# Moving the 64-feature products of the first batch's first MLP half next to the second batch's recurrent groups

## The chip, the core and the metric

The kernel runs on one core of a Trainium2 chip. The metric is the device time of one execution in microseconds (us), as the median of several runs. Engines are named as in the profile: PE is TensorE (matrix products), PEld its weight loads, DVE is VectorE, ACT is ScalarE, POOL is GpSimd, SP is SyncE (here it issues all DMAs).

## The reference

For four batches of 768 tokens, an mLSTM cell with 8 heads of 40 features runs over the tokens and gives x (768 x 320 for each batch). Then x goes through a Fourier mix, a normalization and an MLP with a residual:

```python
C = f_stab * C + i_stab * outer(v, k)          # per head, token by token
n = f_stab * n + i_stab * k
y = sigmoid(o) * (C @ q) / max(|n . q|, 1)     # x: the heads side by side
u = x + real(fft(fft(x, axis=1), axis=2))
un = (u - mean(u)) / sqrt(var(u) + 1e-6)
out = u + max(un @ w_ch1, 0) @ w_ch2           # 320 -> 1280 -> 320
```

All of it is float32. The change concerns `un @ w_ch1` of the first batch only.

## The kernel before, in words

**Recurrence.** The token loop is rewritten into chunks of 128 tokens (6 to a batch); within a chunk all is matrix products, masks and scales, and a small state passes from chunk to chunk. From the second batch on, a chunk is worked as two halves of 64 tokens, with products on 64x64 quarters of the array (line 519, a helper, issues all of them). For chunk c of a batch that starts at slot s0, with s = s0 + 3c, the products stand in this order:

- slot s: `halves_scores` (keys by queries) and `halves_to_state` (what the chunk adds to the state, tile ps). The DVE adds these to the state in `halves_add` (L665, L667).
- slot s+3: `halves_from_state` and `halves_from_chunk(..., 0)` (tile ph); then `halves_between` (L699), a one-element copy by ACT that reads ph; then `halves_from_chunk(..., 1)`, the other half of those products, which PE starts only when that copy is done.

Slot s+3 of chunk c is slot s of chunk c+1, so from the second chunk on the products of two chunks stand together on PE. The text calls such a bunch a recurrent group. Between them `halves_weigh` (L672) has DVE multiply scores by the weights W, which ACT exponentiates (L491) and POOL masks (L515). `mlstm_finish` (L712 to L720, DVE) and `mlstm_tanh` (L605, ACT) end a chunk.

**Fourier mix.** `mix_feat` (L938) makes the mixed features in the tile pu, `mix_add` (L952 to L966, DVE) adds them, `mix_center` (L974, ACT), `mix_turn` (L981, PE transposes) and `mix_turn_out` (L986, ACT) give uT, the features by tokens. `mix_rstd` and `mix_rstd_step` (L994 to L1008) find 1/sqrt(var) on DVE and POOL.

**First MLP half of the first batch.** A group `gr` is 384 tokens (two groups), and f counts ten blocks of 128 hidden features. A product has 320 input features: 128, 64 and 128. The two products over 128 features fill the array (L1059, in `mlp_in`). The product over the 64 middle features fills half of its rows; for two neighbouring f (a pair, n = f // 2) the two run on the upper and the lower half of the rows (L1050, in `between`, inside `mlp_in`). Each float32 product is two instructions in the profile. A pair needs two PSUM banks (tile pm), and `mlp_relu` (L1074, ACT) empties them into h. `bank` hands out four PSUM banks by a written list (`turn`), in the order of requests; pu, put (the transposes), pm and po (the second MLP half, L1184) take from it.

In gr 0, `between` follows each pair's other products. In gr 1, the 64-feature products of pairs 1 and 3 are issued ahead, together with those of pairs 0 and 2.

**Weights.** w1 and w2 arrive as 64-bit floats in pieces (raw) and are converted: DVE splits the words (L406, L408), ACT scales them (L413, L414), DVE joins them (L420 to L426). These conversions stand in the queues of DVE and ACT among the other work of the stretch.

**What sets the order.** A plan: `at(slot, phase, function, ...)` collects the calls, and they are issued sorted by slot and then by phase (EVAC 0, FILL 1, MAIN 2, FILL_PE 3, plus fractions). Each engine takes its instructions in that order and waits on semaphores. For the first batch's MLP, slot 31 + 10 gr + f holds `mlp_in(gr, f)` at MAIN, and the second batch's chunks start at slots 32, 35, 38, 41, 44 and 47. With FILL_PE, the recurrent group of a slot stands after that slot's `mlp_in`. The last chunk's first part stands at MAIN - 0.1 of slot 50, ahead of `mlp_in(1, 9)`.

Of the kernel before, what the change touches and what calls it, by code (L numbers as in the profile page):

```python
# [14 lines left out]
AF = mybir.ActivationFunctionType  # L15
# [4 lines left out]
L = 128  # L20
# [8 lines left out]
NFF = DFF // L  # L29
TAIL = DM - 2 * L  # L30
TG = NT // 2
# [22 lines left out]
def kernel(  # L54
# [14 lines left out]
    nc = tc.nc  # L69
# [18 lines left out]
    def bank(name, shape, n=None):  # L88

        return ps_m.tile(shape, FP, name=name, tag=f"pm{next(turn) if n is None else n}")  # L90
# [14 lines left out]
    w1_sb = const.tile([L, 2, DFF], FP, name="w1_sb")  # L105
    w1t_sb = const.tile([L, DFF // 2], FP, name="w1t_sb")
    w2_sb = const.tile([L, NFF, DM], FP, name="w2_sb")
    uT_bufs = [const.tile([L, 3, TG, L], FP, name=f"uT{n}") for n in range(2)]
# [15 lines left out]
    def at(slot, phase, fn, *args):  # L124
        plan.setdefault((slot, phase), []).append((fn, args))
# [7 lines left out]
    EVAC, FILL, MAIN, FILL_PE = range(4)  # L133
# [248 lines left out]
    class Piece:  # L382
        def __init__(self, dst, src):
            self.dst, self.src, self.float = dst, src, src.dtype == FP
# [377 lines left out]
    def plan_halves(b, s0, stride=3):  # L762
        for c in range(NT):
            s = s0 + stride * c
            t = 22 + 2 * c if b == 1 and c < 3 else s - 5
            at(t, FILL, mlstm_load, b, c)
            at(t, FILL, mlstm_load_max, b, c)
            at(34 if b == 1 and c == 2 else t + 1, FILL, mlstm_load_decay, b, c)
            at(s - 1, FILL, mlstm_load_o, b, c)
            at(s - 1, FILL, mlstm_scale_v, b, c)  # L770
            at(s - 1, FILL + 0.3, mlstm_exp, b, c, 0)
            at(s, FILL, mlstm_exp, b, c, NP)
            at(s, FILL_PE + 2.05, halves_scores, b, c)
            at(s, FILL_PE + 2.5, halves_to_state, b, c)
            for i in range(2):
                at(s + i, FILL + 0.05, halves_decay, b, c, i)
                at(s + 1 + i, FILL - 0.2, halves_add, b, c, i)
            at(s, FILL + 0.1, mlstm_scale_q, b, c)
            at(s + 1, FILL, mlstm_mask, b, c)
            if (b, c) == (3, 2):  # L780
                at(s + 2, MAIN + 0.1, halves_weigh, b, c)
            else:
                at(s + 1, FILL + 0.55 if b == 1 and c > 0 else MAIN + 0.7, halves_weigh, b, c)
            end = c == NT - 1
            at(s + 3, MAIN - 0.1 if end else FILL_PE, halves_from_state, b, c)
            at(s + 3, MAIN - 0.1 if end else FILL_PE, halves_from_chunk, b, c, 0)
            at(s + 3, MAIN if end else FILL_PE + 0.5, halves_between, b, c)
            at(s + 3, FILL_PE + 3, halves_from_chunk, b, c, 1)
            at(s + 3, FILL_PE + 0.6, mlstm_tanh, b, c)
            at(s + (5 if (b, c) == (2, 2) else 4), {(2, 4): FILL + 0.3, (3, 3): FILL - 0.3}.get((b, c), FILL + 0.3 if b == 1 else MAIN + 0.55), mlstm_finish, b, c)  # L790
            at(s + 6, FILL - 0.6, halves_rows, b, c)
# [3 lines left out]

    class Mix:
        def __init__(self):
            self.pu, self.uc, self.pt, self.po = {}, {}, {}, {}

    mixes = {}  # L800

# [239 lines left out]
    def mlp_in(b, gr, f):  # L1041


        k = mixes[b]
        u = [uT_bufs[gr][:, ch].rearrange("p c t -> p (c t)") for ch in range(3)]

        def between(pm, n, start):
            for i in range(2):
                r = slice(i * TAIL, (i + 1) * TAIL)
                nc.tensor.matmul(pm[i], w1t_sb[r, n * L:(n + 1) * L], u[1][r], start=start, stop=not start,  # L1050
                                 skip_group_check=True)


        ahead = gr == 1 and f // 2 in (1, 3)
        if f % 2 == 0:
            k.pm = k.pm_next if ahead else [bank("pm", [L, TG * L]) for _ in range(2)]
        for i, ch in ((1, 1),) if f % 2 else ((0, 0), (0, 1), (1, 0)):
            f0 = (f // 2 * 2 + i) * L
            nc.tensor.matmul(k.pm[i], w1_sb[:, ch, f0:f0 + L], u[2 * ch], start=(ch == 0 and not ahead),  # L1059
                             stop=(ch == 1 and ahead), skip_group_check=True)  # L1060
        if f % 2 and not ahead:
            between(k.pm, f // 2, False)
            if gr == 1 and f // 2 < NFF // 2 - 1:
                k.pm_next = [bank("pm", [L, TG * L]) for _ in range(2)]
                between(k.pm_next, f // 2 + 1, True)


    hid = {}
# [1 line left out]
    def hidden(gr, f):  # L1070
        return hid[gr, f % 2][:, f // 2 * TG * L:(f // 2 + 1) * TG * L]

    def mlp_relu(b, gr, f):
        nc.scalar.activation(out=hidden(gr, f), in_=mixes[b].pm[f % 2], func=AF.Relu, scale=-1.0)  # L1074

# [193 lines left out]
    def plan_mlp(b, s):  # L1271
        groups = range(NT // TG)
        for i in range(NFF // 2) if b > 0 else ():
            for step in range(4):
                at(s, MAIN, mlp_block, b, i, step)
                s += 1
            end = i == NFF // 2 - 1
            for n, (gr, f) in enumerate(((1, 2 * i + 1), (1, 2 * i), (0, 2 * i))):
                at(*((s - 1, MAIN + (-0.1 if gr else 0.1)) if end else (s + n, MAIN + 0.5)), mlp_relu_in_place, gr, f)
        for gr in groups if b == 0 else ():  # L1280
            for f in range(NFF):
                at(s, MAIN, mlp_in, b, gr, f)
                s += 1
                if f % 2:
                    at(s, EVAC, mlp_relu, b, gr, f - 1)
                    at(s, EVAC, mlp_relu, b, gr, f)
        if b > 0:
            for j in range(1, 5):
                at(s - (5, 4, 3, 3)[j - 1], FILL_PE + 0.3, hidden_sums, 0, (j,), 0, NFF // 2 - 2)
            at(s, EVAC, hidden_sums, 0, (1, 2), NFF // 2 - 2, NFF // 2)  # L1290
            at(s, MAIN + 0.1, hidden_sums, 0, (3, 4), NFF // 2 - 2, NFF // 2)
        for n in range(TG) if b > 0 else ():
            for step in range(4):
                at(s, MAIN, mlp_out_pair, b, n, step)
                if n < TG - 1 and step > 1:
                    for j in (2 * step - 3, 2 * step - 2):
                        at(s, MAIN + 0.6, hidden_sums, n + 1, (j,))
                s += 1
        for gr in groups if b == 0 else ():
            for n, (half, i) in enumerate(((0, 0), (0, 1), (0, 2), (1, 0), (1, 1), (1, 2)) if gr == 0 else  # L1300
                                          ((0, 0), (1, 0), (0, 1), (1, 1), (0, 2), (1, 2))):
                at(s, MAIN, mlp_out, b, gr, i, half)
                s += 1
                if half == 1:
                    at(s, EVAC, mlp_store, b, gr, i)
# [6 lines left out]
    def plan_batch(b, s_mlstm, s_mix, s_mlp):  # L1312
        (plan_halves if b > 0 else plan_mlstm)(b, s_mlstm)
        done = [s_mlstm + n for n in ((16, 19, 22) if b == 0 else (18, 21, 22))]
        assert s_mix >= done[-1] and s_mlp >= s_mix + 9
        late = [s_mlp + 2 * c for c in range(TG)]
        if b == 0:
            feat = [s_mix + 1, s_mix + 1, s_mlp + 3]
            turn = [s_mix + 2, s_mix + 3, s_mix + 4]
            add = turn + [s_mlp, s_mlp + 4, s_mlp + 5]  # L1320
            late = [s_mlp + 2, s_mlp + 5, s_mlp + 7]
        else:
            feat = [s_mix + c for c in ((3, 4, 6) if b == 1 else (3, 4, 7))]
            add = [s_mix + c for c in ((4, 4, 5, 6, 7, 7), (4, 5, 5, 6, 8, 9), (4, 4, 5, 6, 8, 9))[b - 1]]
            turn = [s_mix + c for c in ((5, 6, 6) if b == 1 else (6, 7, 8))]
            late = [s_mix + c for c in ((7, 8, 8) if b == 1 else (9, 10, 10))]
            at(s_mlp, EVAC + 0.5, mlp_sums, 0, 3 if b == 2 else 4)
            if b == 2:
                at(s_mlp + 1, MAIN + 0.6, mlp_sums, 3, 4)
        plan_mix(b, s_mix, done, feat, add, turn + late)  # L1330
        s = s_mlp + NFF + 2
        at(s, FILL + 0.6, mix_rstd, b)
        for n in range(3):
            at(s + 3 * n if b == 0 else s, FILL + 0.65, mix_rstd_step, b)
        plan_mlp(b, s_mlp)

    s_mlp = 31
# [154 lines left out]
```

## Time and profile before

| | |
|---|---|
| median of 3 runs | 391.72 us (391.14 to 392.08) |
| the profiled execution | 392.19 us, its span 390.4 us |
| granted TensorE clock | 0.999 |
| PE busy | 379.6 us, 97% of the span |
| DVE, ACT, POOL busy | 278.0, 172.1, 134.9 us |
| L1059, 80 instructions | 59.5 to 110.1 us, 486 ns median |
| L1050, 40 instructions | 62.3 to 111.0 us, 483 ns median |
| L519 of chunks 0 to 5 of batch 2 | in the same stretch |

The span is from the first to the last instruction of the profiled execution; the time of an execution holds a little more. The profile's times are in us from the start of the span. A row of the timeline gives the start, the time up to the last end in the row, the engine, the line and operation, the tiles as out<-in, the shape and the number of instructions; in square brackets stands how long the engine was idle before the row and what ended that. Durations of products overlap, since they are pipelined: how long they hold the array is read from the starts.

### The profile page before, as it was taken

The page shows a single profiled execution, that of the slowest core. Times are in us where ns is not written, and L with a number is a line of the kernel's source. Part 1 is how long each engine was busy: PE and PEld are TensorE (multiplying, and loading weights), DVE is VectorE, ACT ScalarE, POOL GpSimd, SP SyncE. Part 2 cuts the span into 40 slices and gives each one's busy share as a digit, 9 for nine tenths or more (in the row PEclk, how much of TensorE's full clock was granted, in tenths as well). Part 3 has the DMA queues.
Part 4 walks back from the last instruction along what each step waited for, and adds up shares of the span by engine and source line. Part 5 has one row for each costly group of instructions (what it writes and reads, how often), then busy time and mean ns, then how long its engine had stood idle before and what let it go on. Part 6 is the DMA issues. An engine that isn't in the chain of part 4 may idle for free.

```text
span 390.4 us, 10585 instructions
## 1 busy us (share of the span) xinstructions
PE 379.6 (97%) x4174; PEld 277.3 (71%) x4174; DVE 278.0 (71%) x671; ACT 172.1 (44%) x481; POOL 134.9 (35%) x237
## 2 busy tenths in 40 slices
PE   8999899999999999999999999999999999999996
PEld 6777555656667777765569998755588996556996
DVE  7789988499599587476975699777655785346652
ACT  6887357477543233655462314554530133545000
POOL 5739504467954442173254134541500000020000
PEclk9999999999999999999999999999999999999999
DMA  7887499579394345437700626400000000000101
GB/s 224 287 235 204 159 254 255 179 214 271 109 231 116 122 116 150 149 102 184 182 2 28 174 80 192 135 20 2 0 2 34 6 30 34 2 0 0 35 34 35
DMA packets 25631, 44.78 MB, mean 115 GB/s; under 512 B 5727, under 2 KB 14766, under 8 KB 25454
## 3 DMA queue, kind: packets, MB, share of 16 engines
q1 hardware_dynamic: 25582, 44.11, 38.9%
q8 instruction: 33, 0.54, 0.6%
q14 instruction: 16, 0.13, 0.1%
HBM read 38.49 MB, written 4.12 MB: 109 GB/s over the span
## 4 chain that ended last, share of the span: by engine, by line
PE 78%; DVE 14%; issue 3%; ACT 3%; POOL 1%; DVEq 0%; ACTq 0%; POOLq 0%
PE po L1240 20%; PE pm L1121 15%; PE po L1184 8%; PE pm L1059 7%; PE ph L519 4%; PE pm L1126 4%; PE pu L938 4%; PE ps L519 3%; PE pm L1050 2%; PE put L981 2%; PE pz L907 1%; PE pz L895 1%; DVE h L1130 1%; DVE so L716 1%; PE pM L221 1%
## 5 line engine op out<-in xcount | busy, mean ns | idle before, releaser
L1190 DVE SCALAR_TENSOR_TENSOR x<-po,rstd,x 128x160 f32<-128x160 f32 (+1 forms) x69 | 27.1, 394 | 37.4 <-PE po L1240 32.5
L1130 DVE TENSOR_TENSOR h<-h,pm 128x384 f32<-128x384 f32 x60 | 30.5, 548 | 27.1 <-PE pm L1121 12.6
L652 POOL TENSOR_TENSOR C<-C,decB 128x164 f32<-128x164 f32 x30 | 15.9, 531 | 67.5 <-DVE C L667 56.1
L1121 PE MATMUL pm<-uT,w_sb 128*128 128x384 f32 x90 | 37.7, 506 | 1.3 <-DVE uT L1109 0.6
L491 ACT ACTIVATE W<-W,colT 128x64 f32<-128x64 f32 x144 | 37.5, 339 | 0.4 <-DMA W<-M_d 0.4
L1184 PE MATMUL po<-w_sb,h 128*128 128x320 f32 x120 | 34.3, 435 | 0.0
L515 POOL TENSOR_SCALAR_AFFINE_SELECT W<-W 64x512 f32<-64x512 f32 x36 | 27.3, 759 | 10.6 <-ACT W L491 9.1
L1005 POOL TENSOR_TENSOR t<-rstd 128x6 f32<-128x6 f32 x12 | 3.3, 273 | 79.9 <-DVE v L999 79.4
L1059 PE MATMUL pm<-uT,w_sb 128*128 128x384 f32 x80 | 29.2, 500 | 0.1
L1184 PEld LDWEIGHTS po<-w_sb,h 128*128 128x128 f32 x120 | 22.3, 190 | 9.5 <-issue 0.6
L1240 PE MATMUL po<-T,S 128*128 128x160 f32 x180 | 27.8, 301 | 0.3 <-DVE x L1190 0.3
L501 POOL TENSOR_TENSOR qg<-qk,Gb 128x512 f32<-128x512 f32 (+1 forms) x21 | 27.1, 1290 | 1.7 <-DMA qk<-in_qkT 1.6
L1240 PEld LDWEIGHTS po<-T,S 128*128 128x128 f32 x180 | 25.5, 190 | 1.7 <-DVE x L1190 0.5
L1121 PEld LDWEIGHTS pm<-uT,w_sb 128*128 128x128 f32 x90 | 15.5, 189 | 15.6 <-DVE h L1130 6.7
L1240 PE MATMUL po<-w_sb,h 128*128 128x160 f32 x180 | 26.3, 300 | 0.0
L1240 PEld LDWEIGHTS po<-w_sb,h 128*128 128x128 f32 x180 | 25.2, 190 | 1.4 <-DVE x L1190 0.3
L986 ACT COPY uT<-put 128x384 f32<-128x384 f32 x24 | 11.2, 477 | 30.1 <-PE put L981 30.1
L507 POOL TENSOR_TENSOR vw<-kvt,colT 128x328 f32<-128x328 f32 x23 | 19.7, 859 | 13.1 <-DMA qk<-in_qkT 10.1
L1177 ACT ACTIVATE h<-h 128x384 f32<-128x384 f32 x45 | 23.1, 520 | 2.0 <-DVE h L1130 2.0
L1126 PE MATMUL pm<-uT,w1t_sb 64*128 64x384 f32 x120 | 23.4, 508 | 0.0
L1059 PEld LDWEIGHTS pm<-uT,w_sb 128*128 128x128 f32 x80 | 14.1, 189 | 9.6 <-issue 1.9
L974 ACT ACTIVATE uc<-x 128x384 f32<-128x384 f32 x24 | 14.4, 613 | 12.6 <-DVE x L966 11.1
(241 smaller groups left out, 843.4 us busy)
## 6 DMA issues: line engine op xcount, KB each, us to landing
kvt<-in_kv SPq DMA_DIRECT2D x24, 336.0 KB
qk<-in_qkT SPq DMA_DIRECT2D x48, 160.0 KB
raw<-in_w SPq DMA_DIRECT2D x10, 640.0 KB
Gb<-G_d SPq DMA_DIRECT2D x36, 128.0 KB
W<-M_d SPq DMA_DIRECT2D x36, 128.0 KB
so<-in_o SPq DMA_DIRECT2D x24, 160.0 KB
out<-x SPq DMA_DIRECT2D x24, 160.0 KB
x<-so SPq DMA_DIRECT2D x9, 140.0 KB
```

The source lines that it names most:

```text
L491: nc.scalar.activation(out=k.W[:, h, :], in_=M, func=AF.Exp, scale=-1.0, bias=colT[:, c, 0, b * H + h:b * H + h + 1])
L501: nc.gpsimd.tensor_tensor(out=k.qg[:, :, t], in0=k.qk[:, 0, :, t], in1=k.Gb[:, :, t], op=OP.mult)
L515: nc.gpsimd.affine_select(out=W, in_=W, compare_op=OP.is_ge, fill=0.0, base=base, pattern=[[0, H], [step, LH]], channel_multiplier=-1)
L519: nc.tensor.matmul(out, w, x, start=start, stop=True, skip_group_check=True)
L1059: nc.tensor.matmul(k.pm[i], w1_sb[:, ch, f0:f0 + L], u[2 * ch], start=(ch == 0 and not ahead), stop=(ch == 1 and ahead), skip_group_check= ...
L1121: nc.tensor.matmul(bank, w, u, start=start, stop=True, skip_group_check=True)
L1126: nc.tensor.matmul(bank, block(w1t_sb, i)[rows], mlp_u(gr, 1)[rows], start=False, stop=True, skip_group_check=True)
L1130: nc.vector.tensor_tensor(out=h, in0=h, in1=bank, op=OP.add)
L1177: nc.scalar.activation(out=h, in_=h, func=AF.Relu, scale=-1.0)
L1184: nc.tensor.matmul(k.po[gr, i], hidden(gr, f)[:, i * L:(i + 1) * L], w2_sb[:, f, :], start=(f == 0), stop=(f == NFF - 1))
L1190: nc.vector.scalar_tensor_tensor(out=u, in0=po, scalar=k.rstd[:, c:c + 1], in1=u, op0=OP.mult, op1=OP.add)
L1240: nc.tensor.matmul(po, a[:, f], w[:, f], start=start and f == 0, stop=f == half - 1, skip_group_check=True)
```

## The change

The function `between` leaves `mlp_in`, and a new function `mlp_tails(b, gr, n)` issues the four instructions of one pair. Ten entries in the plan place them: pair 0 of gr 0 in slot 32 after `mlp_in` as before; pair 1 of gr 0 in slot 32 after the recurrent products; pair 2 in slot 35, pair 3 in slot 38, pair 4 of gr 0 and pair 0 of gr 1 in slot 41, pairs 1 and 2 of gr 1 in slot 44 and pair 3 in slot 47, each after that slot's `mlp_in` and ahead of its recurrent group; pair 4 of gr 1 in slot 50. In slot 50 the first part of the last chunk's products moves behind `mlp_in(1, 9)`, so that the order is that product, the recurrent products, `halves_between`, the 64-feature products, and the second recurrent part. The relus of blocks 8 and 9 of gr 0 move from slot 41 to slot 42. The start and stop flags follow the new order in each pair. The order in which PSUM banks are asked for stays the same, though pair 1 of gr 0 now asks in slot 32.

```diff
             end = c == NT - 1
-            at(s + 3, MAIN - 0.1 if end else FILL_PE, halves_from_state, b, c)
-            at(s + 3, MAIN - 0.1 if end else FILL_PE, halves_from_chunk, b, c, 0)
-            at(s + 3, MAIN if end else FILL_PE + 0.5, halves_between, b, c)
+            at(s + 3, (MAIN + 0.02 if b == 1 else MAIN - 0.1) if end else FILL_PE, halves_from_state, b, c)
+            at(s + 3, (MAIN + 0.02 if b == 1 else MAIN - 0.1) if end else FILL_PE, halves_from_chunk, b, c, 0)
+            at(s + 3, (MAIN + 0.03 if b == 1 else MAIN) if end else FILL_PE + 0.5, halves_between, b, c)
...
-        def between(pm, n, start):
-            for i in range(2):
-                r = slice(i * TAIL, (i + 1) * TAIL)
-                nc.tensor.matmul(pm[i], w1t_sb[r, n * L:(n + 1) * L], u[1][r], start=start, stop=not start,
-                                 skip_group_check=True)
-
-
-        ahead = gr == 1 and f // 2 in (1, 3)
-        if f % 2 == 0:
-            k.pm = k.pm_next if ahead else [bank("pm", [L, TG * L]) for _ in range(2)]
+        if f % 2 == 0 and (gr, f // 2) not in k.pm:
+            k.pm[gr, f // 2] = [bank("pm", [L, TG * L]) for _ in range(2)]
+        pm, ahead, tailed = k.pm[gr, f // 2], (gr, f // 2) in TAILS_AHEAD, (gr, f // 2) in TAILS_BEHIND
         for i, ch in ((1, 1),) if f % 2 else ((0, 0), (0, 1), (1, 0)):
             f0 = (f // 2 * 2 + i) * L
-            nc.tensor.matmul(k.pm[i], w1_sb[:, ch, f0:f0 + L], u[2 * ch], start=(ch == 0 and not ahead),
-                             stop=(ch == 1 and ahead), skip_group_check=True)
-        if f % 2 and not ahead:
-            between(k.pm, f // 2, False)
-            if gr == 1 and f // 2 < NFF // 2 - 1:
-                k.pm_next = [bank("pm", [L, TG * L]) for _ in range(2)]
-                between(k.pm_next, f // 2 + 1, True)
+            nc.tensor.matmul(pm[i], w1_sb[:, ch, f0:f0 + L], u[2 * ch], start=(ch == 0 and not ahead),
+                             stop=(ch == 1 and not tailed), skip_group_check=True)
+
+    TAILS_AHEAD, TAILS_BEHIND = ((0, 1), (1, 2)), ((0, 0), (0, 3), (0, 4), (1, 1), (1, 4))
+
+    def mlp_tails(b, gr, n):
+
+        k = mixes[b]
+        ahead, last = (gr, n) in TAILS_AHEAD, (gr, n) in TAILS_BEHIND
+        if ahead:
+            k.pm[gr, n] = [bank("pm", [L, TG * L]) for _ in range(2)]
+        for i in range(2):
+            r = slice(i * TAIL, (i + 1) * TAIL)
+            nc.tensor.matmul(k.pm[gr, n][i], w1t_sb[r, n * L:(n + 1) * L], uT_bufs[gr][r, 1].rearrange("p c t -> p (c t)"),
+                             start=ahead, stop=last, skip_group_check=True)
...
                 if f % 2:
-                    at(s, EVAC, mlp_relu, b, gr, f - 1)
-                    at(s, EVAC, mlp_relu, b, gr, f)
+                    late = gr == 0 and f == NFF - 1
+                    at(s + late, EVAC, mlp_relu, b, gr, f - 1)
+                    at(s + late, EVAC, mlp_relu, b, gr, f)
+        if b == 0:
+            for slot, phase, gr, n in ((1, 0.05, 0, 0), (1, 4.5, 0, 1), (4, 0.05, 0, 2), (7, 0.05, 0, 3), (10, 0.05, 0, 4),
+                                       (10, 0.05, 1, 0), (13, 0.05, 1, 1), (13, 0.05, 1, 2), (16, 0.05, 1, 3), (19, 0.05, 1, 4)):
+                at(s_mlp + slot, MAIN + phase, mlp_tails, b, gr, n)
```

More of the change, by code (lines that the diff above doesn't have):

```diff
@@ L797, in __init__ @@
         def __init__(self):
-            self.pu, self.uc, self.pt, self.po = {}, {}, {}, {}
+            self.pu, self.uc, self.pt, self.po, self.pm = {}, {}, {}, {}, {}
     mixes = {}
@@ L1073, in mlp_relu @@
     def mlp_relu(b, gr, f):
-        nc.scalar.activation(out=hidden(gr, f), in_=mixes[b].pm[f % 2], func=AF.Relu, scale=-1.0)
+        nc.scalar.activation(out=hidden(gr, f), in_=mixes[b].pm[gr, f // 2][f % 2], func=AF.Relu, scale=-1.0)
     def block(t, n):
```

## The prediction

> **What bounds the kernel.** I read the busy times first. TensorE is busy for 97% of the span, and no wait of it in the changed stretch exceeds 0.50 us. What the change saves is therefore TensorE time, unless another queue then becomes late.
>
> ```profile
> PE 379.6 (97%) x4174; PEld 277.3 (71%) x4174; DVE 278.0 (71%) x671; ACT 172.1 (44%) x481; POOL 134.9 (35%) x237
> ```
>
> Next came TensorE's timeline of the stretch, 59.5 to 111.7 us (columns: start, time to the last end, engine, line, operation; the next row's start tells when the array was free). L1059 are the 128-feature products, two instructions each; L1050 the 64-feature ones; L519 the recurrent groups.
>
> ```profile
> 66.60 0.81 PE L1059 MATMUL pm<-uT,w_sb 128*128 128x384 f32 x2
> 67.34 0.92 PE L1050 MATMUL pm<-uT,w1t_sb 64*128 64x384 f32 x4
> 68.19 1.35 PE L938 MATMUL pu<-dd_sb,Z 128*128 128x321 f32 x4
> ...
> 79.41 0.92 PE L1050 MATMUL pm<-uT,w1t_sb 64*128 64x384 f32 x4
> 80.25 0.68 PE L519 MATMUL ph<-C,qg 40*64 40x41 f32 x32
> ...
> 82.48 0.44 PE L519 MATMUL ph<-kvt,W 64*64 64x41 f32 x16 [0.50 <-ACT warm L699]
> ...
> 91.72 1.56 PE L1050 MATMUL pm<-uT,w1t_sb 64*128 64x384 f32 x8
> 93.22 2.85 PE L1059 MATMUL pm<-uT,w_sb 128*128 128x384 f32 x8
> ```
>
> From start to next start, four L1050 instructions take 0.85 us and eight take 1.50: four more cost 0.65, so a run has 0.20 us that no instruction accounts for. The L1059 runs agree: x6 takes 2.13 (70.65 to 72.78), x8 2.77 (93.22 to 95.99), 0.32 each and 0.20 per run. Each change between 128-row products, 64-feature products and recurrent groups costs about 0.20 us.
>
> The bracket at 82.48 is the one wait worth following. The timelines of DVE and ACT show its cause:
>
> ```profile
> 74.63 0.33 DVE L667 TENSOR_TENSOR C<-C,ps 128x164 f32<-128x164 f32 x1 [2.64 <-PE ps L519]
> ...
> 75.57 0.49 DVE L958 TENSOR_TENSOR x<-x,pu 128x320 f32<-128x320 f32 x1
> ...
> 78.95 0.48 DVE L406 TENSOR_SCALAR e<-raw 128x640 uint32<-128x640 uint32 x1
> ...
> 79.47 0.83 ACT L413 ACTIVATE e<-e,ebias 128x640 uint32<-128x640 uint32 x1 [0.34 <-DVE e L406]
> ...
> 81.79 0.60 ACT L974 ACTIVATE uc<-x 128x384 f32<-128x384 f32 x1
> 82.29 0.13 ACT L699 COPY warm<-ph 1x1 f32<-1x1 f32 x1
> ```
>
> DVE idles until TensorE ends the state products of the second batch's chunk 1 (74.50), works through its queue without a gap, and releases ACT's weight conversion at 79.47. ACT is then full until L699, the one-element copy (halves_between) behind which TensorE waits. This is a loop: state products, DVE, ACT, and TensorE again 7.98 us later (82.48 - 74.50). TensorE had only 7.48 us of its own work in between.
>
> At the end of the stretch lies a second loop, through POOL:
>
> ```profile
> 106.85 1.51 POOL L515 TENSOR_SCALAR_AFFINE_SELECT W<-W 64x512 f32<-64x512 f32 x2
> 108.39 0.69 DVE L672 TENSOR_TENSOR W<-ps,W 128x512 f32<-128x512 f32 x1
> 109.52 0.83 ACT L413 ACTIVATE e<-e,ebias 128x640 uint32<-128x640 uint32 x1 [2.02 <-DVE e L406]
> 110.88 0.13 ACT L699 COPY warm<-ph 1x1 f32<-1x1 f32 x1
> 111.36 0.44 PE L519 MATMUL ph<-kvt,W 64*64 64x41 f32 x16
> ```
>
> POOL is full from 96.25 to past 108.4; its mask ends at 108.36, DVE starts 0.03 later, and DVE's L406 releases the conversion ahead of L699. TensorE needs L699's end (111.01) at 111.36, so 0.35 us is spare.
>
> **What the Trainium skill says.** TensorEngine Tiling (Array Packing), Key Properties: "Changing tiling mode (not just tile) drains the TensorE". The trace agrees, with the 0.20 us above; 64x128 to 64x64 is a change too (79.41 to 80.25 still takes 0.84), so adjacency halves the cost and doesn't remove it. TensorE: Matmul & The Clock Gate, Part 3: products in different row groups run concurrently. The trace agrees: four L1050 instructions take the array time of two. PSUM — Partial Sum Buffer, Engine vs sequencer instructions: the queues of ScalarE, VectorE and GpSimdE are strictly first in, first out. The trace agrees: L699 waits behind a conversion that has nothing to do with it.
>
> **The change, part by part.** No arithmetic, load or DMA is added or removed; SP's queue keeps its order, as do POOL's and DVE's. The plan's slots, sorted with the new entries, give the new order on each engine.
>
> (1) Runs of 64-feature products. Before there are eight: five between 128-row work on both sides (67.34, 75.50, 85.91, 91.72, 100.72) and three ahead of recurrent work (62.32, 79.41, 110.52). After there are eight, each touching a recurrent group: slot 32 on both sides of the group, and ahead of or within the groups of slots 35, 38, 41 (two pairs), 44 (two pairs), 47, 50. A run on its own costs two changes, beside a group one: five times 0.20 saved. In slot 50 the last 128-row product goes ahead of the group, and group, 64-feature run, group follow directly: one change less. Together 6 x 0.20 = 1.2 us less TensorE work.
>
> The change from recurrent to 64-feature is not in the trace (slots 32, 50). Lower bound 0 (same 64 rows), upper 0.22 (recurrent to 128-row: last start to start 0.16 against 0.04 within the group, and a first instruction 0.10 longer). I take the upper, since the opposite change pays; at 0 another 0.45 would go.
>
> (2) Position. The runs now stand ahead of the groups, so the groups' state products come later although the total is shorter. Shifts of TensorE against before, with 0.85 for a pair's run beside a group, 1.04 for a lone one and 0.65 per further pair:
> - 64.24 (after slot 32): +0.85. At 68.19, the lone run there gone: -0.20.
> - 72.78 (group of chunk 0): +0.65, and with it the state products of chunk 1 (74.50).
> - 76.35 (transposes; the lone run ahead of them counts 1.00, since a transpose loses less on a change): -0.35. At 76.73, slot 37's first product takes the bank that DVE's L958 reads until 76.06; L958 is behind L667, so it now ends at 76.71, and TensorE waits some 0.35 there.
> - 82.48: DVE's and ACT's chain moves by the same +0.65 as L667, since nothing in it idles but for DVE's release. L699 ends at 83.07, and TensorE goes on at 83.13: **+0.65**, by a wait of about 1.1 instead of 0.5.
> - From there: 88.89 +1.10, 93.22 -0.59, 95.99 +0.90, 102.21 -0.79, 104.35 +0.06, 111.36 -0.14.
>
> So of 1.2 us about 1.0 goes to the first loop: 0.65 by which its release is late and 0.35 that TensorE would have been ahead. Had the run stayed behind the group, the wait would still have eaten what it saved.
>
> (3) The second loop. DVE's lag of 0.65 reaches L999 at 96.1 and through it POOL's full queue. DVE catches up at 106.03, where it idled 2.12 us for TensorE; POOL doesn't. Its mask ends at 109.0, L672 starts at 109.04, L406 at 109.65, the conversion at 110.17, and L699 ends at 111.66. TensorE would be there at 111.22 and goes on at 111.71: **+0.35** at 111.36. The 0.85 us of 64-feature products between the group's two parts is cover for L699, but before there was 0.84 us of L1059 as well.
>
> (4) The last relus of the first half move one slot later, behind L699 and the tanh in ACT's queue. The bank that they free is wanted at 92.73, and they end at 91.9 and 92.3, with the second bank wanted 1.4 us later: nothing. They no longer stand ahead of L699 of chunk 2, which is spare there. Banks: the order of requests is unchanged, so every tile keeps its number. The other first uses are preceded by the release by 0.3 us or more.
>
> (5) Behind the stretch. DVE, 0.65 late, must deliver the last w2 rows (L426, 122.01, now 122.7) and the fold (L822, 124.49, now 125.14); TensorE at +0.35 asks for them at 123.15 and 125.53. DVE idles at 128.72 for 1.4 us, and the lag ends. After that all moves with TensorE.
>
> Sum: -1.19 + 1.05 + 0.49 = +0.35 us. The profiled span of 390.40 becomes 390.75. The profiled execution was 392.19, 1.79 more than its span and 0.47 above the median 391.72, which I shift by the same: 392.07.
>
> **The rivals.**
> A, above: 392.1. For it: both loops show in the trace with their releases. Against: it stacks a lag through three queues for 36 us.
> B, POOL or DVE recovers before 108: only the first loop acts, -0.14, 391.6. For: DVE has 1.7 us of idle at 100.29. Against: that idle ends by POOL, which has none.
> C, the saving survives: 390.5, or 390.1 if recurrent to 64-feature is free. This needs ACT or DVE to have room that the timeline doesn't show, so that L699 does not move with 74.63. For: TensorE is the bound everywhere else. Against: the wait at 82.48.
> D, slower: the shared port. POOL's L1005 to L1007 took 0.78, 0.66 and 0.81 us beside long DVE operations (96.25) and 0.20, 0.20, 0.23 beside an idle DVE (104.16). The skill's SBUF — State Buffer, Terms, has VectorE and GpSimd hold that port pair exclusively. If the second step meets long DVE work, POOL's mask is up to 1.6 us later again, and so is L699 at 111.66: 393.7. It makes the kernel measurably slower from 0.43 us of further lag. Against: in my table DVE is idle from 104.6 to 106.1, while those steps run at 104.8.
> E, that nothing changes: excluded, the orders differ.
>
> **Numbers.** A 0.45, B 0.15, C 0.22, D 0.18. About 0.2%, 0.78 us, is what a measurement can tell. A spreads over 391.6 to 392.7 and gives about 0.05 to slower; B is within; C gives 0.22 to faster, with 0.02 from B's and A's lower tail; D all but 0.01 to slower. Faster 0.24, same 0.54, slower 0.22. The range cuts off about half of C and half of D, 390.7 to 393.0; as both signs count, A's own range is 391.6 to 392.7.
>
> **What would show it.** L1050 in eight runs, each beside L519; runs of L1059 x14 without a break; TensorE's idle time ahead of L519 at about 83.1 up to 1 us or more, released by L699, and about 0.35 ahead of L1059 at 76.7 released by DVE's L958; DVE's L667 at 75.28; a wait of 0.5 ahead of the last L519 x16. If TensorE's wait at 83.1 is under 0.5, C is right; if the wait at 111.7 is missing, B; if POOL's second L1005 takes 0.7, D.

## The result, and the profile after

The changed kernel takes 392.49 us (median of 20 runs, 391.46 to 393.88) against 391.75 us (20 runs, 391.12 to 392.35) for the kernel before on the same chip. The medians lie 0.74 us apart. The ratio is 1.0017, with a 95% interval of 1.0009 to 1.0025: 0.67 us more, between 0.35 and 0.98. By the bound that the prediction set, 0.2%, this counts as no change, though it is on the slow side and the interval reaches past the bound. The profiled execution has a span of 390.8 us (before 390.4).

In the changed kernel the products over 128 features are L1052, the 64-feature products L1065, the relu L1075 and the second MLP half L1185.

The busy times of the kernel after, first:

```profile
PE 378.3 (97%) x4174; PEld 277.3 (71%) x4174; DVE 277.8 (71%) x671; ACT 172.0 (44%) x481; POOL 135.4 (35%) x237
```

TensorE is busy for 1.3 us less with the same 4174 instructions, and yet the span is longer. TensorE's timeline of the kernel after, at the places that the prediction named:

```profile
63.41 0.63 PE L519 MATMUL ps<-vw,kvt 64*64 64x41 f32 x32
63.97 0.92 PE L1065 MATMUL pm<-uT,w1t_sb 64*128 64x384 f32 x4
64.81 2.20 PE L1052 MATMUL pm<-uT,w_sb 128*128 128x384 f32 x6
...
76.59 2.82 PE L1052 MATMUL pm<-uT,w_sb 128*128 128x384 f32 x8 [0.31 <-DVE x L958]
...
82.86 0.44 PE L519 MATMUL ph<-kvt,W 64*64 64x41 f32 x16 [0.95 <-ACT warm L699]
...
83.61 4.68 PE L1052 MATMUL pm<-uT,w_sb 128*128 128x384 f32 x14
...
109.98 0.92 PE L1065 MATMUL pm<-uT,w1t_sb 64*128 64x384 f32 x4
111.54 0.44 PE L519 MATMUL ph<-kvt,W 64*64 64x41 f32 x16 [0.64 <-ACT warm L699]
```

The 64-feature products stand beside the recurrent groups, and the 128-feature ones come in runs of up to fourteen instructions without a break. In exchange three waits stand in brackets where before there was one, of 0.50 us: behind DVE's L958, and twice behind ACT's one-element copy L699. Two sums of TensorE's waits of the kernel after (columns: total, times, longest, us):

```profile
PE ph L519 <- ACT warm L699: 1.9, 3, 1.0
...
PE pz L907 <- POOL fe L822: 0.6, 1, 0.6
```

Before, they were 0.8 us in 2 waits and 0.2 us in 1. One wait of 0.3 us behind L699 lies outside of the changed stretch in both kernels. The row of L907 is no effect of the change: this wait ends at 47.75 us (at 48.02 before), ahead of all changed code, and takes anything from 0.11 to 0.65 us in the profiled kernels. The cause of the two waits behind L699 stands in the timelines of DVE, ACT and POOL of the kernel after:

```profile
75.01 0.32 DVE L667 TENSOR_TENSOR C<-C,ps 128x164 f32<-128x164 f32 x1 [3.48 <-PE ps L519]
...
75.95 0.49 DVE L958 TENSOR_TENSOR x<-x,pu 128x320 f32<-128x320 f32 x1
...
106.05 0.33 DVE L667 TENSOR_TENSOR C<-C,ps 128x164 f32<-128x164 f32 x1 [1.77 <-POOL C L652]
...
108.87 0.69 DVE L672 TENSOR_TENSOR W<-ps,W 128x512 f32<-128x512 f32 x1 [0.74 <-POOL W L515]
```

```profile
79.85 0.83 ACT L413 ACTIVATE e<-e,ebias 128x640 uint32<-128x640 uint32 x1 [1.34 <-DVE e L406]
...
82.67 0.13 ACT L699 COPY warm<-ph 1x1 f32<-1x1 f32 x1
...
111.35 0.13 ACT L699 COPY warm<-ph 1x1 f32<-1x1 f32 x1
```

```profile
104.51 0.20 POOL L1005 TENSOR_TENSOR t<-rstd 128x6 f32<-128x6 f32 x1
...
107.20 1.64 POOL L515 TENSOR_SCALAR_AFFINE_SELECT W<-W 64x512 f32<-64x512 f32 x2
```

The reader sees the same two loops as before, later: DVE's L667 waits for TensorE until 75.01 and hands its lateness down to ACT's L413 and L699; POOL's mask ends at 108.84, DVE's L672 starts 0.03 us later, and L699 follows at 111.35.

**A common scale.** Work ahead of the changed code ends at slightly different times in different executions: the first product of the first MLP half starts at 59.54 us before, at 59.27 after, and between 58.0 and 59.5 in the experiments, none of which touches anything earlier. So positions are compared relative to that product. I call the time from it to the fifth product of the second batch's first MLP half (L1121 before, at 165.17 us) the **stretch**: 105.63 us before, 106.21 after, +0.58. What lies behind differs by 0.03 us. The first L1121 product (at 163.48 before) lies 1.68 or 1.69 us ahead of the fifth in every kernel. From the first L1184 product to it, the stretch's second half, it is 51.74 or 51.75 us in twelve of the fourteen profiled kernels and 51.88 in the other two, so a difference of a tenth in a stretch can be read. Each stretch is of one execution. The ratios compare runs that were taken together, so they are not exactly the quotients of the medians. A wait under 0.15 us gets no bracket in a timeline, so "no wait" below means none longer than that.

On this scale the shifts are: L667 of chunk 1 +0.65 us; L699 behind it and TensorE's resumption +0.65; L699 of the last chunk +0.74, TensorE +0.44; at the fold of the second batch +0.58, which stays to the end. The fold is what DVE's L815 to L827 make of x for the Fourier mix; L907 are TensorE's products on it, and the shift is that of the fourth of them.

### The profile page after: what moved, and what is told of

The parts are those of the page before. It is cut to its first block, busy times and chain, and to the rows that moved or that the text cites. A ratio compares the mean times of both kernels' runs of the same rounds, so it can differ in the third digit from the quotient of the medians.

```text
span 390.8 us, 10585 instructions
## 1 busy us (share of the span) xinstructions
PE 378.3 (97%) x4174; PEld 277.3 (71%) x4174; DVE 277.8 (71%) x671; ACT 172.0 (44%) x481; POOL 135.4 (35%) x237
## 4 chain that ended last, share of the span: by engine, by line
PE 76%; DVE 14%; issue 3%; ACT 3%; POOL 2%; DMA 1%; DVEq 0%; POOLq 0%; ACTq 0%; SPq 0%
PE po L1241 20%; PE pm L1122 15%; PE po L1185 8%; PE pm L1127 4%; PE pu L938 4%; PE ph L519 3%; PE pm L1052 3%; PE ps L519 3%; PE put L981 2%; PE pz L907 1%; PE pz L895 1%; DVE so L716 1%; PE ph L560 1%; PE ph L553 1%; PE pM L221 1%
## 5 line engine op out<-in xcount | busy, mean ns | idle before, releaser
L652 POOL TENSOR_TENSOR C<-C,decB 128x164 f32<-128x164 f32 x30 | 15.9, 529 | 67.1 <-DVE C L667 48.2
L1122 PE MATMUL pm<-uT,w_sb 128*128 128x384 f32 x90 | 37.7, 506 | 1.3 <-DVE uT L1110 0.6
L1185 PE MATMUL po<-w_sb,h 128*128 128x320 f32 x120 | 34.3, 435 | 0.0
L515 POOL TENSOR_SCALAR_AFFINE_SELECT W<-W 64x512 f32<-64x512 f32 x36 | 27.7, 770 | 12.4 <-ACT W L491 11.1
L1005 POOL TENSOR_TENSOR t<-rstd 128x6 f32<-128x6 f32 x12 | 3.3, 272 | 80.0 <-DVE v L999 79.4
L1185 PEld LDWEIGHTS po<-w_sb,h 128*128 128x128 f32 x120 | 22.2, 190 | 9.6 <-issue 0.6
L1052 PE MATMUL pm<-uT,w_sb 128*128 128x384 f32 x80 | 28.2, 496 | 0.4 <-DVE x L958 0.3
L501 POOL TENSOR_TENSOR qg<-qk,Gb 128x512 f32<-128x512 f32 (+1 forms) x21 | 27.5, 1311 | 2.3 <-DMA Gb<-G_d 1.8
L1122 PEld LDWEIGHTS pm<-uT,w_sb 128*128 128x128 f32 x90 | 15.5, 189 | 15.6 <-DVE h L1131 6.7
L507 POOL TENSOR_TENSOR vw<-kvt,colT 128x328 f32<-128x328 f32 x23 | 19.9, 863 | 12.7 <-DMA kvt<-in_kv 10.1
L1052 PEld LDWEIGHTS pm<-uT,w_sb 128*128 128x128 f32 x80 | 14.4, 190 | 10.0 <-issue 0.8
```

The source lines that it names most:

```text
L501: nc.gpsimd.tensor_tensor(out=k.qg[:, :, t], in0=k.qk[:, 0, :, t], in1=k.Gb[:, :, t], op=OP.mult)
L515: nc.gpsimd.affine_select(out=W, in_=W, compare_op=OP.is_ge, fill=0.0, base=base, pattern=[[0, H], [step, LH]], channel_multiplier=-1)
L1052: nc.tensor.matmul(pm[i], w1_sb[:, ch, f0:f0 + L], u[2 * ch], start=(ch == 0 and not ahead), stop=(ch == 1 and not tailed), skip_group_che ...
L1122: nc.tensor.matmul(bank, w, u, start=start, stop=True, skip_group_check=True)
L1185: nc.tensor.matmul(k.po[gr, i], hidden(gr, f)[:, i * L:(i + 1) * L], w2_sb[:, f, :], start=(f == 0), stop=(f == NFF - 1))
```

## The experiments

The theory on trial: TensorE's saving is real, and two loops through the in-order queues of DVE, POOL and ACT take it back, since the conversion of the w2 weights stands in ACT's queue ahead of L699. Each conversion has three calls in the plan: `take` (DVE's L406 and L408), `convert` (ACT's L413 and L414) and `join` (DVE's L420 to L426). The five triples of w2 have slots 36, 39, 42, 48 and 51 for `take`. The rival: TensorE is held anyway, by something else or by the position of the runs.

### Conversions moved to a later slot

If the conversion no longer stands ahead of L699, the loops are cut. The edit moves `convert` by two slots and `join` by one, in the changed kernel and in the kernel before:

```diff
-    when += [((s, 0.7), (s + 1, 0.7), (s + 2, 0.6)) for s in (36, 39, 42, 48, 51)]
+    when += [((s, 0.7), (s + 3, -0.5), (s + 3, 0.6)) for s in (36, 39, 42, 48)]
+    when += [((51, 0.7), (52, 0.7), (53, 0.6))]
```

> The changed kernel with the w2 conversions on ScalarE (L413, L414) and their joins moved three slots on, behind L699, the tanh and the relus. Theory (loop: late state products, VectorE, conversion, L699, TensorE): no wait ahead of L519 at 83 and 111 us; only the 0.35 us ahead of L1052 at 76.6 (VectorE's L958) stays, so 1.19 - 0.35 = 0.84 us under the kernel before, about 390.9, and 1.5 under the changed kernel. Rival (VectorE's full queue is the bound and the waits are only where it shows): no gain, about 392.4, with waits of the same sum elsewhere.

> The kernel before with the same move of the conversions and nothing of the change: the control. Loop: the wait of 0.50 us at 82.48 goes, 391.25. Rival: 391.75, no difference.

In the changed kernel: 393.01 us against 392.0, ratio 1.0045 (1.0028 to 1.0062), stretch 106.70. In the old order: 392.56, ratio 1.0019 (1.0011 to 1.0028), stretch 106.45. No wait for L699 is left in the stretch, in either, but both became slower. TensorE's timeline of the changed kernel with this edit:

```profile
105.52 0.69 PE L519 MATMUL ps<-qk 40*64 40x64 f32 x32 [1.80 <-DVE C L667]
```

And DVE's timeline of the old order with it, at the second of its waits (0.95 us, at 104.64):

```profile
101.48 1.28 DVE L420 SCALAR_TENSOR_TENSOR e<-raw,e 128x640 uint32<-128x640 uint32 x1
...
103.53 0.82 DVE L426 TENSOR_TENSOR w_sb<-m,e 128x640 f32<-128x640 f32 x1
104.27 0.32 DVE L667 TENSOR_TENSOR C<-C,ps 128x164 f32<-128x164 f32 x1
```

An earlier wait behind L667, of 0.35 and 0.36 us, stands in the two orders, and the wait behind L958 stays in the changed order. The join of 2.8 us now stands ahead of L667, the add of the state for which TensorE waits. The next loads of w2 move too, since each is issued a slot after the join two pieces ahead, but no wait of DVE for a load shows. The expectation missed: this cuts one loop and closes another. In the changed kernel with the edit ACT is now idle ahead of the two L699 in question, for 1.24 us (80.69) and 3.00 us (110.97); without it ACT came to them straight from its queue. That ties L699's waits to the conversion; it doesn't show that the saving survives.

### The runs behind their groups

The runs of slots 35 to 47 go behind the recurrent group of their slot, so that the groups' state products are not later than before:

```diff
-            for slot, phase, gr, n in ((1, 0.05, 0, 0), (1, 4.5, 0, 1), (4, 0.05, 0, 2), (7, 0.05, 0, 3), (10, 0.05, 0, 4),
-                                       (10, 0.05, 1, 0), (13, 0.05, 1, 1), (13, 0.05, 1, 2), (16, 0.05, 1, 3), (19, 0.05, 1, 4)):
+            for slot, phase, gr, n in ((1, 0.05, 0, 0), (1, 4.5, 0, 1), (4, 4.5, 0, 2), (7, 4.5, 0, 3), (10, 4.5, 0, 4),
+                                       (10, 4.5, 1, 0), (13, 4.5, 1, 1), (13, 4.5, 1, 2), (16, 4.5, 1, 3), (19, 0.05, 1, 4)):
```

> The changed kernel with the 64-feature runs of slots 35, 38, 41, 44 and 47 behind the recurrent groups and not ahead: as few tiling changes, but the state products are not delayed. Loop: L667 0.20 us earlier than before (in the stretch's own time), L699 likewise, so TensorE's wait at the first loop is about 1.5 us and the whole is 0.2 under before: 391.55, no wait at 111. Rival (position does not matter, the loss is in TensorE or VectorE): like the changed kernel, 392.4.

392.05 us, ratio 1.0004 (0.9994 to 1.0015); stretch 105.89, between before and after. TensorE's timeline of this kernel:

```profile
81.28 0.44 PE L519 MATMUL ph<-kvt,W 64*64 64x41 f32 x16 [1.34 <-ACT warm L699]
```

TensorE resumes 22.73 us after the first product (before 22.94, after 23.59): the position made the first loop late, as argued. TensorE now arrives earlier and waits 1.34 us, so position alone gains nothing on the kernel before. A further wait behind L699, of 0.35 us, appears at 96.37, for chunk 3; the one of the last chunk is gone. So the first wait grew and the last one went, as expected, but the gain of 0.2 us on the kernel before did not come: the stretch is 0.26 longer, with a wait at 96.37 that the expectation did not have.

The same with the later conversions of the first experiment:

> Both: runs behind the groups, conversions moved. Loop: no waits, the whole saving of six tiling changes stays, 1.19 us under before: 390.55. Rival: no gain over the kernel before, 391.7.

392.83 us, ratio 1.002 (1.0012 to 1.0027), stretch 106.75: three waits behind L667, of 0.32, 0.89 and 1.15 us. The expectation missed for the reason seen above.

### The first conversion one slot earlier

DVE idles for 2.64 us ahead of L667 in the kernel before. In the next edit the first piece's `take` goes into that idle time and its `convert` one slot forward, from 37 to 36; `join` stays. Below this is called the early split:

```diff
-    when += [((s, 0.7), (s + 1, 0.7), (s + 2, 0.6)) for s in (36, 39, 42, 48, 51)]
+    when += [((35, 0.2), (36, 0.7), (38, 0.6))]
+    when += [((s, 0.7), (s + 1, 0.7), (s + 2, 0.6)) for s in (39, 42, 48, 51)]
```

> The changed kernel with only the first w2 piece's split (L406, L408) moved one slot earlier on VectorE, into its idle time ahead of L667, and its conversion on ScalarE (L413, L414) ahead of the relus of pair 2; every join stays where it was. Theory (the first loop runs through that split): no wait ahead of L519 at about 82.5, VectorE's lag does not arise, so also no wait at 111.5 and none at the fold; the 0.3 us ahead of L1052 stays. TensorE's stretch from its first 128-feature product to the first mlp_block product becomes 0.8 us shorter than before (105.6 to 104.8), 1.4 than the changed kernel. Rival (VectorE's full queue bounds the stretch, as the runs with moved joins suggest): the waits come back at later L519, the stretch stays at 106.2.

> The kernel before with the same early split: the control. Theory: the wait of 0.50 us at 82.48 goes and no other comes, the stretch 105.1. Rival: 105.6.

> The 64-feature runs behind the recurrent groups and the early split. Theory: neither the loop nor L958 makes TensorE wait, the whole 1.19 us stays: the stretch 104.4, the time 1.2 us under before. Rival: a wait at a later L519 takes it, stretch about 105.6.

| order | us (before: 391.81) | ratio to before | stretch |
|---|---|---|---|
| changed | 390.88 | 0.9976 (0.9969 to 0.9984) | 104.90 |
| old | 390.77 | 0.9978 (0.9971 to 0.9986) | 104.72 |
| behind | 390.80 | 0.9989 (0.9976 to 1.0003) | 104.59 |

(The fourteen runs of the third row go from 389.94 to 393.86.) The wait at 83 us is gone in all three, and the stretch is 1.31, 0.91 and 1.30 us shorter than that of the same order without the edit. ACT's timeline of the changed order shows the conversion out of the way, and idle time ahead of L699:

```profile
75.00 0.81 ACT L413 ACTIVATE e<-e,ebias 128x640 uint32<-128x640 uint32 x1
...
81.15 0.15 ACT L699 COPY warm<-ph 1x1 f32<-1x1 f32 x1 [1.19 <-issue]
```

So ACT's conversion, released by DVE, was what made L699 late. The old order gains 0.4 us more than expected: 0.69 us where the wait of 0.50 was, and 0.20 at chunks 2 and 3, where L699 had also held TensorE, too shortly for a bracket (before, L699 ends at 90.46 and 97.52, and TensorE goes on at 90.51 and 97.57). Each order answers differently at the other end. The old order has no wait left in the stretch. The changed one keeps the wait behind L958, the one of the last chunk and the loss at the fold, against the expectation that the second wait only passed on the lag of the first. The timelines of DVE, ACT and TensorE of the changed order with the edit:

```profile
107.51 0.69 DVE L672 TENSOR_TENSOR W<-ps,W 128x512 f32<-128x512 f32 x1 [0.74 <-POOL W L515]
```

```profile
108.64 0.83 ACT L413 ACTIVATE e<-e,ebias 128x640 uint32<-128x640 uint32 x1 [2.75 <-DVE e L406]
```

```profile
110.18 0.44 PE L519 MATMUL ph<-kvt,W 64*64 64x41 f32 x16 [0.56 <-ACT warm L699]
```

DVE waits for POOL's mask, the fourth conversion comes right behind it, and L699 behind that (110.00): with the first loop cut, TensorE arrives earlier, and the second loop holds it by itself. With the runs behind the groups, the third piece's conversion holds chunk 3 instead. ACT's timeline of that kernel:

```profile
93.15 0.83 ACT L413 ACTIVATE e<-e,ebias 128x640 uint32<-128x640 uint32 x1 [1.01 <-DVE e L406]
```

L699 follows at 95.47, and TensorE waits 0.76 us for it, until 95.65.

### The fourth conversion one slot earlier, alone

```diff
-    when += [((s, 0.7), (s + 1, 0.7), (s + 2, 0.6)) for s in (36, 39, 42, 48, 51)]
+    when += [((s, 0.7), (s + 1, 0.7), (s + 2, 0.6)) for s in (36, 39, 42)]
+    when += [((47, 0.7), (48, 0.7), (50, 0.6)), ((51, 0.7), (52, 0.7), (53, 0.6))]
```

> The changed kernel with only the fourth w2 piece's split and conversion one slot earlier (ahead of the last chunk's L699, so off the second loop). Theory: the first loop is as in the changed kernel (wait of about 0.95 ahead of L519 near 83), the wait near 111.5 (0.64) is gone, and VectorE's lag at the fold too: stretch 105.5 to 105.7, 0.5 to 0.7 less than the changed kernel. Rival: no difference to the changed kernel, 106.2.

As with the first piece, `take` and `convert` move and `join` stays. 391.92 us, ratio 1.0004 (0.9993 to 1.0014); stretch 105.76, or 0.45 less than after, a little under the 0.5 to 0.7 that was expected. The first wait stays (0.95 us at 82.38), the last falls from 0.64 to 0.22 us and is now behind DVE's L672 itself, at 109.53, and the loss at the fold is gone: from the first L1185 product to the first L1122 product it takes 51.75 us, against 51.88 after. The two loops can thus be undone one by one, and in the changed kernel this one costs 0.3 us and the fold 0.1.

### Third conversion behind L699, first and fourth early

Here the third piece's `convert` and `join` go behind L699 (the expectation says that the join stays; it stays in its slot, but behind the products) and the first and fourth conversions are early, in the order with the runs behind the groups and in the old order:

```diff
+    when += [((35, 0.2), (36, 0.7), (38, 0.6)), ((39, 0.7), (40, 0.7), (41, 0.6)), ((42, 0.7), (44, 2.7), (44, 2.8))]
+    when += [((47, 0.7), (48, 0.7), (50, 0.6)), ((51, 0.7), (52, 0.7), (53, 0.6))]
```

> Runs behind the groups, the first split early, the third piece's conversion behind the chunk's L699 (its join stays), the fourth split early: no conversion stands ahead of an L699 that TensorE waits for. Theory: no wait of TensorE in the stretch beyond 0.2 us; against the run with the runs behind and the early split only (104.6, with 0.95 us lost at one L519) the stretch is 0.9 shorter, 103.7; 1.9 under the kernel before. Rival: VectorE or GpSimd bounds it, a new wait, 104.5.

> The same moves of split and conversion in the kernel before, nothing of the change: the control that prices the six tiling changes without a wait. Theory: as with the early split alone (104.7), since that had no wait left; so 1.0 to 1.2 us above the run that has the 64-feature runs behind the groups. Rival (the change of order is worth nothing even then): within 0.3 us of that run.

Runs behind: 391.47 us, ratio 0.9995 (0.9984 to 1.0006), stretch 104.99. Old order: 392.05, ratio 1.0007 (0.9993 to 1.0021), stretch 105.57. Both missed, by 1.3 and 0.9 us of stretch. DVE, POOL and TensorE of the first of the two:

```profile
97.47 2.79 DVE L426 TENSOR_TENSOR w_sb<-m,e 128x640 f32<-128x640 f32 x1
```

```profile
96.71 1.04 POOL L652 TENSOR_TENSOR C<-C,decB 128x164 f32<-128x164 f32 x1
```

```profile
102.61 0.68 PE L519 MATMUL ph<-C,qg 40*64 40x41 f32 x32 [1.32 <-POOL t L1005]
```

The late join meets POOL's full queue. It begins only at 95.42, since DVE idles 1.15 us for the conversion. POOL's L652 took 0.46 us at this place in the kernel after and takes 1.04, L732 ahead of it 0.93 instead of 0.44, and DVE's L426 takes 2.79 (the same join took 0.83 at 98.10 in the kernel after). TensorE then waits 1.32 us for POOL: the bracket names L1005, but of POOL's work just ahead of it the operand of this group is vw, which L507 finishes at 102.27. In the old order the waits are 0.31 us for POOL's L507 and 0.22 for DVE's L672. Against the early split alone (104.59 and 104.72) the stretches are 0.40 and 0.85 us longer: a conversion moved later is the wrong way here too, by another path than in the first experiment.

### Both early, and one run behind its group

The first and fourth conversions early in the changed order, and then with the run of slot 35 alone put behind its group, so that the state products of chunk 1, L667 and L958 come earlier:

```diff
+    when += [((35, 0.2), (36, 0.7), (38, 0.6)), ((39, 0.7), (40, 0.7), (41, 0.6)), ((42, 0.7), (43, 0.7), (44, 0.6))]
+    when += [((47, 0.7), (48, 0.7), (50, 0.6)), ((51, 0.7), (52, 0.7), (53, 0.6))]
```

```diff
-            for slot, phase, gr, n in ((1, 0.05, 0, 0), (1, 4.5, 0, 1), (4, 0.05, 0, 2), (7, 0.05, 0, 3), (10, 0.05, 0, 4),
+            for slot, phase, gr, n in ((1, 0.05, 0, 0), (1, 4.5, 0, 1), (4, 4.5, 0, 2), (7, 0.05, 0, 3), (10, 0.05, 0, 4),
```

> The changed kernel as it is, 64-feature runs ahead of the groups, with the first and the fourth split early. Theory: both loops cut; left are 0.3 us ahead of L1052 (L958) and up to 0.3 us ahead of the last chunk's products (VectorE's L672 behind GpSimd's mask): stretch 104.4 to 104.6, 1.1 under the kernel before, against 104.9 with the first split alone. Rival: no better than 104.9.

> The changed kernel with the first and the fourth split early, and of the 64-feature runs only the one of slot 35 behind its recurrent group, so that chunk 1's state products and with them VectorE's L667 and L958 come 0.85 us earlier. Theory: the wait ahead of L1052 near 77 goes and no other grows, because VectorE's and GpSimd's chains start earlier too: stretch 104.0, against 104.44 with the run ahead of the group; 1.6 under the kernel before. Rival: a later wait (the third conversion ahead of chunk 3's L699, or VectorE's L672 behind GpSimd's mask) takes the difference: 104.4.

Both early: 390.52 us against 391.81, ratio 0.9968 (0.9955 to 0.9981), stretch 104.44, as expected. With one run behind as well: 389.91 (5 runs) against 391.38 (9 runs), ratio 0.9953 (0.9938 to 0.9968), stretch 103.58, 0.4 below what was expected. TensorE's timeline of the former at the place in question, then of the latter:

```profile
76.83 2.82 PE L1052 MATMUL pm<-uT,w_sb 128*128 128x384 f32 x8 [0.31 <-DVE x L958]
```

```profile
76.38 2.75 PE L1052 MATMUL pm<-uT,w_sb 128*128 128x384 f32 x8
...
109.31 0.44 PE L519 MATMUL ph<-kvt,W 64*64 64x41 f32 x16
```

From the transposes ahead of it (at 76.03 and 76.05) to this product it is 0.80 us with the wait and 0.33 without, so the wait had cost 0.47 us and not the 0.31 in its bracket. The last chunk's wait, 0.10 us behind DVE's L672 in the former, is gone as well. Now no wait of TensorE is left in the stretch, and this is the fastest kernel of the study: 1.47 us below the kernel before.

It also gives the worth of the new order by itself, since the old order with the early split has no wait in the stretch either. TensorE's timelines of that old order and of this kernel, from the first product to the first of L1121 (here L1122):

```profile
58.87 2.85 PE L1059 MATMUL pm<-uT,w_sb 128*128 128x384 f32 x8
...
161.91 2.57 PE L1121 MATMUL pm<-uT,w_sb 128*128 128x384 f32 x6
```

```profile
59.53 2.85 PE L1052 MATMUL pm<-uT,w_sb 128*128 128x384 f32 x8
...
161.43 2.57 PE L1122 MATMUL pm<-uT,w_sb 128*128 128x384 f32 x6
```

The stretches are 104.72 and 103.58. The difference is 1.14 us, the TensorE work that the new order saves (the prediction's 1.19). It is from one execution of each, and the old order with the fourth conversion early too was not run; having no wait, it had none to lose by it.

## Why the prediction was right, and where a size was off

The prediction was +0.35 us, no measurable change, by a saving that two loops take back. Measured was +0.74 between the medians and +0.58 in the stretch, by these loops and a small loss behind them.

**Step (1), right.** Six changes at 0.20, 1.19 us: 1.14 us by the two orders without waits, 1.3 by the busy times. The change from recurrent to 64-feature products, which the trace of before didn't show, costs what the upper bound said: in the kernel after it is 0.56 us from the last row of the recurrent group to the run of four (63.41 to 63.97), just as long as from that row to a 128-feature product in the kernel before:

```profile
63.68 0.63 PE L519 MATMUL ps<-vw,kvt 64*64 64x41 f32 x32
64.24 2.20 PE L1059 MATMUL pm<-uT,w_sb 128*128 128x384 f32 x6
```

The run itself takes 0.84 us to the next start (64.81), as beside any other neighbour. So the Trainium skill's sentence on draining (TensorEngine Tiling (Array Packing), Key Properties) fits here also between 64x64 and 64x128 products, which use equally many rows.

**Step (2), right in the loop's end, with waits off by 0.1 to 0.2.** L667, L699 and TensorE at chunk 1 all moved by 0.65 us, as the working had it. (Its "a transpose loses less" is in the trace of before: three transposes take 0.38 us from start to next start behind a 64-feature run, at 76.35, and 0.32 behind 128-feature products, at 66.28.) The wait behind the transposes came, but TensorE left it later than foreseen: relative to the first product it is 0.13 us late at 76.59 where the working had 0.00, and 0.21 late at the recurrent group (80.19). So the wait for L699 is 0.95 and not 1.1. L699 sets where TensorE goes on, so the sum keeps its 0.65. The early split of the first conversion shows that the chain through L406 and L413 was the cause, and the runs behind their groups bear out the step's last sentence: their position moves the loop's end, and what TensorE saves then goes into a longer wait (1.34 us).

**Step (3), right in mechanism, too small by 0.1.** POOL stayed late, and the last wait cost TensorE 0.44 us of shift instead of 0.35. The mis-sized term is the mask: L515 held POOL for 1.59 us before (106.85 to 108.44) and for 1.72 after (107.20 to 108.92). DVE caught up only in part: at 106.05 it waits for POOL's L652 and not for TensorE, and is 0.29 us late there; this costs nothing, since DVE then waits for the mask anyway. And the second loop is more than an heir of the first, as the early split of the first piece showed: once TensorE comes earlier, POOL's mask and the fourth conversion hold it on their own.

**Step (4), right.** No wait of TensorE for a bank behind the moved relus appears.

**Step (5), the one that failed.** It let a DVE lag of 0.65 pass unnoticed at the fold, with 0.39 us to spare before TensorE asks. On the common scale DVE was 1.11 us late there (L822). DVE's timeline before and after:

```profile
114.00 0.82 DVE L426 TENSOR_TENSOR w_sb<-m,e 128x640 f32<-128x640 f32 x1
...
124.18 0.31 DVE L822 TENSOR_TENSOR fe<-eo 128x159 f32<-128x159 f32 x1
```

```profile
114.48 1.23 DVE L426 TENSOR_TENSOR w_sb<-m,e 128x640 f32<-128x640 f32 x1
...
125.02 0.31 DVE L822 TENSOR_TENSOR fe<-eo 128x159 f32<-128x159 f32 x1
```

The join takes 0.41 us longer. POOL's timelines say what else ran, before and after:

```profile
114.91 0.72 POOL L501 TENSOR_TENSOR qg<-qk,Gb 128x256 f32<-128x256 f32 x1 [1.63 <-DMA qk<-in_qkT]
```

```profile
114.12 0.91 POOL L501 TENSOR_TENSOR qg<-qk,Gb 128x256 f32<-128x256 f32 x1 [0.36 <-DMA kvt<-in_kv]
```

Before, POOL's L501 started behind the join; after, its data came earlier, and it was running when the join started. In six of the fourteen profiled kernels this join starts while POOL runs L501 or L507, and takes 1.23 or 1.24 us; in the other eight POOL is idle when it starts, and it takes 0.82 or 0.83. That is the shape of the port that DVE and POOL share (the Trainium skill, SBUF — State Buffer, Terms: either engine holds it exclusively), which rival D had placed elsewhere; the pattern is shown, the port as its cause is argued. The loss at the fold is small: the step from the third to the fourth L907 product is 0.43 us from start to start after, against 0.32 before, and ahead of it the load of weights waits 0.5 us for DVE's L822. POOL's start hangs on the landing of a transfer, so this 0.1 need not be there in every execution.

**The sum.** Predicted +0.35; in the trace +0.58, which is -1.14 of work and, as the remainder, 1.72 of waits. Of the 0.23 between them 0.09 is from step (3) and 0.14 lies behind the first L1185 product (51.88 against 51.74): 0.11 of it at the fold, and 0.03 in the L1185 products ahead of the fold, which I can't place. The interval of the ratio, 0.35 to 0.98 us, holds the 0.58 and ends at the predicted 0.35; no further cause is called for, and it shows none either.

**The rivals.** B (POOL recovers) falls with the wait at 111.54. C (the saving survives) needed room in DVE and ACT that isn't there: L699 moved by just what L667 did. Where the room was made, by two earlier conversions and one run put back, the saving survived in full. D falls in the place it named: POOL's second L1005 took 0.20 us, not 0.7.

## What to carry to other kernels

A short wait of the bound engine can be the end of a loop through the queues of engines that are busy for less of the span (here ACT, 44%). A reordering that saves work on the bound engine but issues the loop's first product later gave its gain to that wait: follow the product's consumer through each queue to the wait before pricing the saving. The remedy is to take unrelated work out of the loop towards idle time ahead of it; moved later it met the next consumer's deadline here in every trial. With that done, and one run put behind its group, the reordering was worth 1.14 us of its 1.19.

## What the runs showed of the hardware that was not expected

- The waits in brackets ahead of a product understate what the array lost here. With the first conversion's split early, the wait of 0.95 us vanished from the changed kernel, and TensorE was 1.14 us earlier; in the old order 0.50 vanished and 0.69 came back; the one of 0.31 behind L958 had cost 0.47. So 0.16 to 0.19 us of each wait lies under the end that the profile gives the product before it; these ends are modelled.
- The same DVE join took 0.82 us or 1.23, going with whether a POOL operation was running when it started (eight and six of fourteen kernels); beside a full POOL queue another join of the same form took 2.79.
- The end of the work ahead of the changed code varied by 1.5 us between profiled executions of kernels that are equal up to there. A common starting point inside the stretch was needed to read differences of a tenth.
